# Long sums in 64-row tiles, in two passes with the row halves swapped

## The chip, the cores and the metric

The kernel runs on one core of one Trainium2 chip. Its time is that of one execution on the device, in microseconds (us); given is the median over several executions. TensorE (PE) does the matrix products, ScalarE (ACT) and VectorE (DVE) empty its results and do the rest of the arithmetic with GpSimd (POOL), and SyncE (SP) issues transfers.

## What is computed

One transformer block over 2048 tokens of width 448, with the layer norms modulated by a condition vector. All data are bf16.

```python
mod = (_silu(c) @ w_mod).reshape(...)            # six vectors of 448: sa, ca, ga, sb, cb, gb
h = _layernorm(x) * (1 + ca) + sa
q, k, v = h @ wqkv                               # 16 heads of 28
idx = pos[:, None] - 2 * arange(8)               # each token sees itself and 7 others, every second one back
attn = softmax(where(idx >= 0, q . k[idx] / sqrt(28), -1e9))
x = x + ga * ((attn . v[idx]) @ wo)
h = _layernorm(x) * (1 + cb) + sb
y = _layernorm(h)
x = x + gb * (gelu(y @ w1 + b1) @ w2 + b2)       # 448 -> 1792 -> 448
```

## The kernel before

**Tiles and stages.** The tokens lie as eight token tiles `p` of 128 partitions x 2 tokens (`NS = 2`). Tiles 0 and 1 are normalised first and go through a short start; for tiles 2 to 7 `natural_qk` (L614 to 632) computes K and then Q with the tokens on partitions, ScalarE casts the result into a staging tile `zy` (L628), and a DMA transpose issued by SP brings it into `kT` or `qT` (L631). The attention (`attention`, L678 to 797) runs over nine batches `i`: V (`pv`), the logits `lt` (L738) in two halves, the exponential `et`, the denominator `pd` (L760) and the weighted sum `po` (L771). V of batches 0 to 4 is computed straight from the normalised tokens (L706), of batches 5 to 8 from a copied window `hw`. `out_proj(p)` (L797, matmuls L803, result `pw`) is followed by the second layer norms and by a transpose into `yT` (L834). `mlp(t)` (L845 to 894) works on two token tiles at a time: w1 gives `p1` in PSUM, ScalarE's GELU (L864) writes `hm`, w2 (L883) sums 14 feature tiles into `p2`, L889 adds the residual and L893 stores. The whole is done in three phases: attention batches 0 to 4 and `mlp(0)`, batches 5 and 6 and `mlp(1)`, batches 7 and 8 and `mlp(2)` and `mlp(3)`, with work of neighbouring phases interleaved.

**Sums over 448.** The contraction of Q, K, V and w1 is 448 = 3 x 128 + 64 rows (`KT = 4` steps, `KS = 64`). `summed` (L543) adds two tasks for its items: `full`, three matmuls over all 128 rows for every item (L548), and `rest`, the half step (L554), in which two items run side by side, one on rows 0 to 63 of the array and one on rows 64 to 127 (`tile_position`). The output projection contracts 4 x 128 rows, w2 14 x 128. w1 uses `summed` for two groups `g` at a time, each with two items. On TensorE a change between such tile shapes (128 rows x 128 columns, 64 x 128, 64 x 64, 32 x 64 and so on) is called a change of tile shape below.

**What sets the order.** The program is first recorded as numbered tasks (`Plan.add`) with their dependences, and then emitted in the order of the list `ORDER`; an entry like `29:A` sends a task to another engine. `SLOTS` gives each buffer its place in the pools of `ROOM`; the PSUM pool `P` has four places of two banks. Each engine executes its instructions in the order in which they were emitted. SP carries all loads, the transposes (L527 for the normalised tokens `zT`, L631, L834) and the stores, in one sequence.

Of the kernel before, what the change touches and what calls it, by code (L numbers as in the profile page):

```python
# [14 lines left out]
S, D, H, DH, F = 2048, 448, 16, 28, 1792  # L15
KT, KS = 4, 64
# [4 lines left out]
NS = 2  # L21
SL = S // NS
LEAD = 16
# [16 lines left out]
DIRECT = range(0, 5)  # L40
ENGINE = {"A": "ACT", "D": "DVE", "P": "POOL", "R": "PE2"}
RATE = 310e3
SLOTS = [
# [10 lines left out]
85 90:A 93:P 36 114 94+3@94 82 95 113 102 92:A 91 115:D 86 103 116 96 120:A 144 97 99 104 106 117:A 135 98 118:A 142  # L54
105 119:A 145 143 133 100 146 121 136 134 126 148 137 107 147 7 127 149:D 122 138 124 150 129 139 190 123 191 140 198
141 128 125 200 199 269 130 271 236 40 270 207 33 209 38 241 201 35 237 208 210 185 211 154 39 153 242 202 152 212
151:A 8 203 187 213 238 204 159 239 214:D 205 215 186 240 155 278 206 188 279 280 156 160 307:R 161 281 243 37 282 272
192 273:A 162 157 189 171 308:D 194 172 283 193 244 218 173 195 163 219 158 275 284 196 216 285 167 217 286 447:P 246
197 164 168 165 228 174 169:D 274 309 312 276:D 277 220 313 310 314 166 221 229 225 230 311 224 222:D 247 170 315 245
176 317 316 175 226 248 233 232 318 227 290 249 289:A 319 43 287:A 223 288 320 234 250 558:P 46 45 559 321 47 231 253  # L60
345 342 346 251 560 303 482:P 44 252 324 343 322 291 561 254 323 325 347 326 344 292 304 255 293 327 348 328 373:R 256
305 294 329 257 350 258 375 52 378 376 330 340:R 53 333 379 235 377 374 296 334 331 300 41 295 351 332 259 49 335 380
299 341 336 337 297 260 382 262 301 381 349 263 261 264 338:A 383 483 352 339 384 265 484 266 449 353 267 485 385 268
# [3 lines left out]
402 452 404 443 487 453 370 490 454 444 436 455 371:D 372 456 434 491 405 488 457 493 445 459 458 492 460 435 494 461  # L67
# [3 lines left out]
513 547 515:D 599 516 564 602 568 481 569 570 604 603 571 546 605 572 548 606 573 628 607 608 574 549 635 575 550 609  # L71
612 636 577 630 637 578 610 629 640 576 579 638 581 639 611 613 580 582 641 631 583 633 586 651 614 632 587 584 585
616 588 642 615 648 617 654 646 647 618 634 652 645 656 621 649 619 644 622 620 623 643 658 650 625 624 589 626 664
590 655 627 591:A 653 657 439 592 659 556 665 662 663 674 666 660 661 669 667 675 668 678 676 679 677 686 672 673 671
687 681 670 680 690 691 694 697 693 682 688 692 685 695 683 689 701 684 698 696 709 699 710 702 711 712 705 700 703
706 704 707 708
# [77 lines left out]
def kernel(  # L154
# [14 lines left out]
    nc = tc.nc  # L169
# [3 lines left out]
    P = Plan()  # L173
    add = P.add
# [19 lines left out]
    qT = cst.tile([128, 4 * NS, WT], BF16, name="qT")  # L194
# [45 lines left out]
    first = []  # L240
# [301 lines left out]

    def summed(items, slot, reads, bufs, fills, name, after=(), split=None):  # L543
# [70 lines left out]
    def natural_qk(p):  # L614
        c0 = LEAD + 128 * p
        for half in (1, 0):
            pq = psum("pq")

            def item(s, half=half, pq=pq):
                return (lambda: pq.t[:, s, 0:D], lambda kt, rows: hT[rows, NS * kt + s, c0:c0 + 128],  # L620
                        lambda kt, rows: (wqk_st.t[:, kt] if kt < KT - 1 else wqr_st.t[rows])[:, half * D:half * D + D])
# [174 lines left out]

    def out_proj(p):  # L797
        pw = psum("pw")

        def mm():  # L800
            for s in range(NS):
                for ft in range(4):
# [160 lines left out]
```

## Time and profile before

| | |
|---|---|
| median of 3 executions | 170.32 us (169.31 to 171.79) |
| profiled execution: span | 166.6 us (its whole time is not recorded) |
| PE busy, matmuls | 160.9 us (97%), 2126 |
| PE weight loads | 83.7 us (50%) |
| DVE, ACT, POOL busy | 116.1, 102.4, 46.7 us |
| granted TensorE clock | 0.9 of full speed or more in all 40 slices |
| DMA | 18.78 MB, mean 113 GB/s |

The span is the time from the first to the last instruction of the profiled execution; the times of the executions hold what lies around it too. In the rows of the profile `L548 PE MATMUL p<-yT,w_s` is a matmul of line 548 that writes the tile `p` (buffer numbers are left out, so `p1` and `p2` read `p`) from `yT` and `w_s`; a shape `128*128 128x512` is the rows and columns of the array's tile, then the moving operand. `A <- B: 0.5, 1, 0.5` in a list of waits means that A waited for B for 0.5 us in all, once.

### The profile page before, as it was taken

What the parts mean: (1) busy time and instruction counts of PE and PEld (TensorE: products, weight loads), DVE (VectorE), ACT (ScalarE), POOL (GpSimd) and SP (SyncE); (2) the same over time, 40 slices, a digit from 0 to 9 for tenths busy, and PEclk for the clock granted to TensorE, in tenths of its full rate; (3) what the DMA queues carried; (4) which work ended last, traced back from release to release, by engine and by line L of the source; (5) the groups of instructions that cost most, each with busy time, mean ns of one, the idle gap of its engine ahead of it and who ended that gap; (6) DMA issues with size and microseconds to landing.
All of it is one profiled execution on the core that took longest, in us unless ns stands there. A gap on an engine that the chain in (4) does not pass through costs nothing.

```text
span 166.6 us, 4971 instructions
## 1 busy us (share of the span) xinstructions
PE 160.9 (97%) x2126; PEld 83.7 (50%) x2126; DVE 116.1 (70%) x271; ACT 102.4 (61%) x142; POOL 46.7 (28%) x73
## 2 busy tenths in 40 slices
PE   6999899999999999999999999999999999999992
PEld 4678544444545543445555344556434455344572
DVE  6889899958899989996938886574788930500032
ACT  3378898798489953859674468947536820097300
POOL 3136332300261201289100114700002870007200
PEclk9999999999999999999999999999999999999999
DMA  5999989799999999900091000009010026110003
GB/s 152 323 335 311 182 269 172 147 160 190 222 185 306 147 161 245 151 0 6 2 139 46 4 0 0 4 0 126 8 55 0 0 55 185 64 46 0 0 1 110
DMA packets 35573, 18.78 MB, mean 113 GB/s; under 512 B 28507, under 2 KB 34592, under 8 KB 35552
## 3 DMA queue, kind: packets, MB, share of 16 engines
q1 hardware_dynamic: 35548, 18.47, 51.0%
q8 instruction: 16, 0.26, 0.7%
q14 instruction: 5, 0.04, 0.1%
q10 hardware_dynamic: 4, 0.00, 0.0%
HBM read 9.81 MB, written 1.84 MB: 70 GB/s over the span
## 4 chain that ended last, share of the span: by engine, by line
PE 88%; DMA 4%; ACT 2%; SPq 2%; POOL 1%; DVE 1%; issue 1%
PE p L883 26%; PE p L548 22%; PE pq L548 8%; PE pw L803 8%; PE pv L706 5%; PE p L554 4%; PE lt L738 4%; PE po L771 3%; PE pv L548 3%; DMA wqk_st<-in_A_wqkv_dram 3%; PE pq L554 2%; DMA kT<-zy 2%; PE pd L760 1%; SPq L349 1%; PE pb L641 1%
## 5 line engine op out<-in xcount | busy, mean ns | idle before, releaser
L864 ACT ACTIVATE hm<-p,b_col 128x512 bf16<-128x512 f32 x56 | 33.9, 692 | 29.9 <-PE p L554 27.3
L883 PE MATMUL p<-w_s,hm 128*128 128x448 bf16 (+1 forms) x238 | 44.1, 342 | 0.0
L548 PE MATMUL p<-yT,w_s 128*128 128x512 bf16 x168 | 38.1, 380 | 0.0
L469 POOL TENSOR_TENSOR rs_all<-mvs,neg_half 128x2 f32<-128x2 f32 x22 | 16.7, 764 | 58.0 <-DVE mvs L458 57.9
L883 PEld LDWEIGHTS <-hm 128*128 128x128 bf16 x238 | 22.6, 98 | 19.3 <-issue 0.8
L889 DVE TENSOR_TENSOR x_all<-p,x1p 128x896 bf16<-128x896 f32 (+2 forms) x10 | 8.9, 902 | 25.9 <-PE p L883 25.9
L548 PEld LDWEIGHTS <-w_s 128*128 128x128 bf16 x168 | 15.8, 98 | 20.9 <-issue 2.9
L456 DVE BATCH_NORM_STATS2 stt<-x_all 128x6 f32<-128x448 bf16 x32 | 18.6, 608 | 0.8 <-DMA x_all<-in_A_x_dram 0.6
L745 ACT ACTIVATE et<-lt 128x928 bf16<-128x928 f32 x18 | 16.0, 947 | 4.2 <-PE lt L738 3.9
L841 POOL TENSOR_TENSOR x1p<-x_all,gbb_bc 128x448 f32<-128x448 bf16 x16 | 17.8, 1137 | 0.0
L548 PE MATMUL pq<-wqk_st,hT 128*128 128x448 bf16 x72 | 15.0, 354 | 0.0
L788 DVE TENSOR_TENSOR qT<-po,den 128x912 bf16<-128x912 f32 x9 | 10.0, 1106 | 6.6 <-ACT den L782 6.4
L751 DVE TENSOR_TENSOR et<-et,mask 128x928 bf16<-128x928 bf16 x18 | 11.8, 683 | 3.1 <-ACT et L745 3.0
L803 PE MATMUL pw<-wo_s,qT 128*128 128x448 bf16 x64 | 13.3, 353 | 0.0
L780 ACT ACTIVATE den<-pd 128x928 f32<-128x928 f32 x9 | 8.5, 943 | 5.9 <-PE pd L760 5.7
L819 DVE TENSOR_TENSOR h<-h,mod_bc 128x896 bf16<-128x896 bf16 x16 | 11.1, 710 | 0.3
L628 ACT CAST zy<-pq 128x896 bf16<-128x896 f32 x10 | 8.9, 912 | 1.7 <-PE pq L554 0.9
L548 PEld LDWEIGHTS <-hT 128*128 128x128 bf16 x72 | 6.4, 98 | 6.9 <-issue 1.6
L782 ACT ACTIVATE den<-den,den_bias 128x928 f32<-128x928 f32 x9 | 9.6, 1072 | 0.2
L478 DVE TENSOR_SCALAR zy<-h,mvs,rs_all 128x448 bf16<-128x448 bf16 x16 | 6.6, 457 | 4.4 <-POOL rs_all L469 4.4
L810 DVE TENSOR_TENSOR x_all<-pw,x_all 128x896 bf16<-128x896 f32 x8 | 8.7, 1086 | 1.3 <-PE pw L803 1.3
L456 DVE BATCH_NORM_STATS2 stt<-h 128x6 f32<-128x448 bf16 x16 | 9.4, 612 | 0.2
(115 smaller groups left out, 182.0 us busy)
## 6 DMA issues: line engine op xcount, KB each, us to landing
w_s<-in_B_w_dram SPq DMA_DIRECT2D x7, 224.0 KB, 3.8
out_dram<-x_all SPq DMA_DIRECT2D x7, 224.0 KB, 2.1
x_all<-in_A_x_dram SPq DMA_DIRECT2D x3, 448.0 KB, 5.3
wmod<-in_w_mod_dram SPq DMA_DIRECT2D x3, 448.0 KB, 7.2
w_s<-in_B_w_dram SPq DMA_DIRECT2D x3, 448.0 KB
wqk_st<-in_A_wqkv_dram SPq DMA_DIRECT2D x3, 225.0 KB, 3.9
wm_st<-in_w_mod_dram SPq DMA_DIRECT2D x1, 672.0 KB, 4.6
x_all<-in_A_x_dram SPq DMA_DIRECT2D x2, 224.0 KB, 2.6
```

The costliest lines, as they stand in the source:

```text
L456: add("DVE", 0.53, lambda: nc.vector.bn_stats(out=stt[:, w, b, 0:6], in_=src()), reads=reads, bufs=bufs, after=early if w == b == 0 else ( ...
L469: ways = {"POOL": (0.55 + 0.17 * n, lambda: nc.gpsimd.tensor_tensor(out=r, in0=v, in1=neg_half[:, 0:n], op=ALU.pow))}
L548: nc.tensor.matmul(out(), lhsT=lhs(kt, slice(0, 128)), rhs=rhs(kt, slice(0, 128)), start=first and kt == 0, stop=not first and kt == KT - 2)
L554: nc.tensor.matmul(out(), lhsT=lhs(KT - 1, rows), rhs=rhs(KT - 1, rows), start=first, stop=not first, tile_position=(rows.start, 0))
L745: exps.append(add("ACT", 0.83, lambda half=half, lt=lt: nc.scalar.activation(out=et.t[:, 2 * half:2 * half + 2].rearrange("p r m c -> p r ...
L751: nc.vector.tensor_tensor(out=ev, in0=ev, in1=mask[:], op=ALU.mult)
L788: nc.vector.tensor_tensor(out=qT[:, :, LEAD + q00:LEAD + q00 + 2 * WQ], in0=po.t[:, :, 0:NS * 4 * WQ].rearrange("p j (m c) -> p m j c", c=WQ),
L803: nc.tensor.matmul(pw.t[:, s, 0:D], lhsT=qT[:, KT * s + ft, LEAD + 128 * p:LEAD + 128 * p + 128], rhs=wo_s[:, ft, :], start=(ft == 0), sto ...
L819: add("DVE", 0.55, lambda vec=vec, op=op: nc.vector.tensor_tensor(out=h2.t[:], in0=h2.t[:], in1=vec.unsqueeze(1).to_broadcast([128, NS, D] ...
L841: add("POOL", 1.0, lambda n=n: nc.gpsimd.tensor_tensor(out=x1p.t[:, n, :], in0=xn(p, n), in1=gbb2_bc[:], op=ALU.add), reads=[f"x{p}", "gbb ...
L864: gelus.append(add("ACT", 0.585, lambda f=f, a=a, p1=p1s[g]: nc.scalar.activation(out=hm.t[:, f].rearrange("p n c -> p (n c)"), in_=p1.t[: ...
L883: nc.tensor.matmul(p2.t[:, n, 0:c1 - c0], lhsT=hm.t[:, f, n, q * 128:(q + 1) * 128], rhs=w2_s[:, f, c0:c1], start=(f == parts[0][0]), stop ...
```

## The change

For Q and K of token tiles 2 to 7, V of batches 5 to 8, all output projections, all of w1, and w2 of token tiles 0 to 6, every matmul now uses 64 rows. Two items share the array: in the first pass item 0 has the upper row halves and item 1 the lower ones, in the second they are swapped. Where the contraction is 448, the half step is part of the first pass (four steps, then three). Between the passes SP executes an instruction `nop`, the hop, that waits for the last matmul of the first pass, and the first matmul of the second pass waits for the hop. w1 is recorded for each group `g` alone. w2 of the last token tile stays as it was. `ORDER` is new from its third line on, `SLOTS` from the middle of its first.

```diff
+PAIRED_QK, PAIRED_V, PAIRED_WO, PAIRED_W2 = range(2, 8), range(5, 9), range(0, 8), range(0, 7)
-85 90:A 93:P 36 114 94+3@94 82 95 113 102 92:A 91 115:D 86 103 116 96 120:A 144 97 99 104 106 117:A 135 98 118:A 142
+85 90:A 93:P 36 114 94+3@94 82 95 113 102 92:A 91 115:D 86 103 116 96 120:A 144 97 99 104 106 117:A 135 7 8 105 119:A
...
+    def swapped(first, bufs, second):
+        ends = []
+        def hop():
+            nop = nc.sync.nop()
+            for mm in ends:
+                link(mm, nop)
+            ends.append(nop)
+        a = first(ends)
+        b = add("SP", 0.05, hop, needs=a, name="hop")
+        return a + second(ends, [b])
...
+    def paired(items, slot, reads, bufs, fills, name, after=(), rest=True):
+        n = KT - 1 if rest else KT
+        seen = []
+        def half(first, ends):
+            start, mm = not seen, None
+            seen.append(1)
+            for kt in range(KT if first else n):
+                for a in range(2):
+                    out, lhs, rhs = items[a if first else 1 - a]
+                    rows = slice(KS * a, KS * a + KS)
+                    mm = nc.tensor.matmul(out(), lhsT=lhs(kt, rows), rhs=rhs(kt, rows), start=start and kt == 0,
+                                          stop=not start and kt == n - 1, tile_position=(rows.start, 0))
+                    if not first and kt == a == 0:
+                        link(ends[-1], mm)
+            if first:
+                ends.append(mm)
...
-            summed([item(s) for s in range(NS)], 0.1895, [f"wqk{k}" for k in range(KT - 1)] + ["wr0", "wr1"] + [f"h{kt}_{p}" for kt in range(KT)],
+            (paired if p in PAIRED_QK else summed)([item(s) for s in range(NS)], 0.1895, [f"wqk{k}" for k in range(KT - 1)] + ["wr0", "wr1"] + [f"h{kt}_{p}" for kt in range(KT)],
...
+        if p in PAIRED_WO:
+            paired([item(s) for s in range(NS)], 0.1895, reads, [pw], [pw], f"wo{p}", rest=False)
...
-            w1_mms.extend(summed([item(g, a) for g in gs for a in range(2)], 0.2160,
...
+            for g in gs:
+                w1_mms.extend(paired([item(g, a) for a in range(2)], 0.2160, [f"w1{k}" for k in (0, 1, 2, "r0", "r1")] + [(yT, 0), (yT, 1)],
+                                     [yT, p1s[g]], [p1s[g]], f"w1_{t}_{g}", after=lts))
...
+                        for f in fs:
+                            for a in range(2):
+                                n, rows = (1 - a if up else a), slice(KS * a, KS * a + KS)
+                                mm = nc.tensor.matmul(p2.t[:, n, 0:D], lhsT=hm.t[rows, f, n, q * 128:(q + 1) * 128], rhs=w2_s[rows, f, :],
+                                                      start=done == 0 and f == fs[0], stop=done == 3 and f == fs[-1], tile_position=(rows.start, 0))
+                                if done == 2 and f == fs[0] and a == 0:
+                                    link(ends[-1], mm)
```

`link(a, b)` makes `b` wait for `a` by a semaphore. Every matmul is preceded by its weight load; there are 2650 matmuls after and 2126 before.

The first place is TensorE at the first w1, the rows in which the last output projection of the first phase (`pw`) ends and w1 begins. Before (one row of each kind; six matmuls for each `p1` on L548, two on L554):

```order
L803 MATMUL pw_1570<-wo_s_75,qT_70 128x448
L548 LDWEIGHTS w1_s_76
L548 MATMUL p1_1587<-yT_1534,w1_s_76 128x512
...
L548 MATMUL p1_1594<-yT_1534,w1_s_76 128x512
L554 LDWEIGHTS w1_r_77
L554 MATMUL p1_1613<-yT_1534,w1_r_77 128x512
...
L554 MATMUL p1_1616<-yT_1534,w1_r_77 128x512
...
L554 MATMUL p1_1587<-yT_1534,w1_r_77 128x512
...
L554 MATMUL p1_1594<-yT_1534,w1_r_77 128x512
```

After (L576 is the matmul in `paired`; eight matmuls for each `p1` in the first pass, six in the second):

```order
L576 MATMUL pw_1689<-wo_s_75,qT_70 128x448
L576 LDWEIGHTS w1_s_76
L576 MATMUL p1_1724<-yT_1632,w1_s_76 128x512
...
L576 MATMUL p1_1724<-yT_1632,w1_r_77 128x512
L576 LDWEIGHTS w1_s_76
L576 MATMUL p1_1736<-yT_1632,w1_s_76 128x512
...
L576 MATMUL p1_1748<-yT_1632,w1_r_77 128x512
L576 LDWEIGHTS w1_s_76
L576 MATMUL p1_1724<-yT_1632,w1_s_76 128x512
```

The runs over 128 rows with their remainders over 64 have become first passes of three groups and then their second passes, all in one tile shape; between the first pass of `p1_1724` and its second stand the first passes of `p1_1736` and `p1_1748`.

The second place is SP, where the first Q and K of the natural layout are made (the names behind `waits` are the semaphores that the row waits for; `zT` and `kT`/`qT` rows are the transposes, `wo_s` a load, `mod_hbm` a small transfer). Before:

```order
L527 DMA_TRANSPOSE zT_615<-zy1_97 128x8x128 [waits DMAHW4_49,DMAHW3_49,DMAHW5_49,DVE_49,Activation_49]
L527 DMA_TRANSPOSE zT_615<-zy0_96 128x8x128 [waits Pool_49]
L366 DMA wo_s_75<-in_A_wo_dram 28x4x448
L631 DMA_TRANSPOSE qT_70<-zy2_98 128x8x128 [waits DMAHW6_49,Activation_49]
L648 DMA mod_hbm_79<-mod_rows_80 4x448 [waits DMAHW7_49,Activation_49]
L631 DMA_TRANSPOSE kT_71<-zy3_99 128x8x128 [waits DMAHW0_49]
```

After:

```order
L531 DMA_TRANSPOSE zT_538<-zy0_96 128x8x128 [waits DMAHW3_49,Pool_49]
L531 DMA_TRANSPOSE zT_538<-zy1_97 128x8x128 [waits PE_49,DMAHW4_49,Pool_49]
L370 DMA wo_s_75<-in_A_wo_dram 28x4x448 [waits PE_49,DMAHW5_49]
L675 DMA_TRANSPOSE qT_70<-zy2_98 128x8x128 [waits DMAHW6_49,Activation_49]
L692 DMA mod_hbm_79<-mod_rows_80 4x448 [waits PE_49,DMAHW7_49,Activation_49]
L675 DMA_TRANSPOSE kT_71<-zy0_96 128x8x128 [waits DMAHW0_49]
```

The hop has no row of its own; it stands ahead of each row that now waits for TensorE as well (`PE_49`). Nothing else in these six rows is moved except which staging tile is transposed first.

The third place is TensorE at the first attention batches, where `pv` of batch 0 is computed. Before, one row of each run:

```order
L738 MATMUL lt_391<-qT_70,kT_71 64x58
L548 MATMUL pq_353<-hT_69,Wqk_72 128x256
L548 MATMUL pq_362<-hT_69,Wqk_72 128x256
L706 MATMUL pv_447<-Wv_74,hT_69 64x448
L738 MATMUL lt_470<-qT_70,kT_71 64x58
```

After:

```order
L782 MATMUL lt_404<-qT_70,kT_71 64x58
L782 MATMUL lt_437<-qT_70,kT_71 64x58
L592 MATMUL pq_374<-hT_69,Wqk_72 128x256
L750 MATMUL pv_483<-Wv_74,hT_69 64x448
L750 MATMUL pv_511<-Wv_74,hT_69 64x448
```

The second half of the logits (`lt_470` before, `lt_437` after) has moved ahead of the first `pv`, and one of the two Q/K runs over 128 rows that stood between the first logits and `pv` now stands ahead of the logits.

More of the change, by code (lines that the diff above doesn't have):

```diff
@@ L58 @@
[L58 to L62, printed above, removed]
@@ L541, in front_ln, with link @@
             affine(u, lambda kt: ptr[kt % 2].t[:, :, kt // 2], [(ptr[0], q) for q in range(np_)], ptr, True)
+    def swapped(first, bufs, second):
[8 more added lines that the diff above has]
+        return a + second(ends, [b])
+    def link(a, b):
+        tc.add_manual_dep(b.ins, a.ins.name, mybir.DependencyInfo(mybir.DependencyClass.Sync, mybir.DependencyReason.DATA), reason="swap")
+    def paired(items, slot, reads, bufs, fills, name, after=(), rest=True):
[14 more added lines that the diff above has]
+                ends.append(mm)
+        both = dict(reads=reads, bufs=bufs, joins=fills, mode="64x128")
+        return swapped(lambda ends: [add("PE", KT * slot, lambda: half(True, ends), instr=4 * KT, name=name + "p", after=after, **both)], bufs,
+                       lambda ends, b: [add("PE", n * slot, lambda: half(False, ends), instr=4 * n, name=name + "q", needs=b, **both)])
     def summed(items, slot, reads, bufs, fills, name, after=(), split=None):
@@ L798, in out_proj, with item @@
         pw = psum("pw")
+        def item(s):
+            return (lambda: pw.t[:, s, 0:D], lambda ft, rows: qT[rows, KT * s + ft, LEAD + 128 * p:LEAD + 128 * p + 128],
+                    lambda ft, rows: wo_s[rows, ft, :])
         def mm():
             for s in range(NS):
+                out, lhs, rhs = item(s)
                 for ft in range(4):
[L803 to L804 removed]
+                    nc.tensor.matmul(out(), lhsT=lhs(ft, slice(0, 128)), rhs=rhs(ft, slice(0, 128)), start=(ft == 0), stop=(ft == 3))
         batches = [i for i in range(NB) if i * SBQ < 128 * (p + 1) and (i + 1) * SBQ > 128 * p]
[L807 to L808 removed]
+        reads = ["wos0", "wos1"] + [f"o{i}" for i in batches]
+        if p in PAIRED_WO:
+            paired([item(s) for s in range(NS)], 0.1895, reads, [pw], [pw], f"wo{p}", rest=False)
+        else:
+            add("PE", 8 * 0.1895, mm, reads=reads, bufs=[pw], fills=[pw], instr=16, name=f"wo{p}")
         xp = x_all[:, p, :].rearrange("p (s d) -> p s d", s=NS)
@@ L890, in mlp @@
                     out=xo(xi), in0=p2.t[:, n0:n1, 0:w], in1=xo(x1p.t), op=ALU.add),
-                    bufs=[p2, x1p], reads=[(p2, n) for n in ns] + [(x1p, n) for n in ns], writes=[f"out{p}{n0}{c0}"] + ([] if last else [f"x{p}"]), name="fin")
+                    bufs=[p2, x1p], reads=[(p2, n) for n in ns if p not in PAIRED_W2] + [(x1p, n) for n in ns], writes=[f"out{p}{n0}{c0}"] + ([] if last else [f"x{p}"]), name="fin")
                 lo, hi = n0 * D + c0, (n1 - 1) * D + c1
```

69 lines of the change are left out of this document (42 added, 27 removed), and 24 rows, old and new, of tables (ORDER, SLOTS).

## The prediction

> **What bounds the kernel now.** I read the head of the page first, then the waits of the engines, then the chain that ended last in order of time.
>
> ```profile
> span 166.6 us, 4971 instructions
> PE 160.9 (97%) x2126; PEld 83.7 (50%) x2126; DVE 116.1 (70%) x271; ACT 102.4 (61%) x142; POOL 46.7 (28%) x73
> PEclk9999999999999999999999999999999999999999
> PE 88%; DMA 4%; ACT 2%; SPq 2%; POOL 1%; DVE 1%; issue 1%
> ```
>
> TensorE (PE) is busy for 160.9 of 166.6 us at a full granted clock, and 88% of the chain is its own work. What it waits for in the whole execution is a short list (columns: total us, times, longest):
>
> ```profile
> PE ps_c L382 <- DVE warm_w L242: 1.3, 1, 1.3
> PE pv L706 <- ACT qT L609: 0.5, 1, 0.5
> PE po L771 <- issue: 0.3, 1, 0.3
> PE pq L562 <- DVE Wqk L439: 0.2, 1, 0.2
> PE ps_col L410 <- ACT silu_bc L398: 0.2, 1, 0.2
> ```
>
> Only the second and the third, 0.8 us together, lie in the part whose order changes. So the time can move in three ways only: how many columns TensorE streams, what it pays between matmuls, and new waits. The chain in order of time (start, length, what), at the first w1 stage, shows what it pays between:
>
> ```profile
> 61.34 1.62 PE pw L803 x8
> 62.96 2.59 PE p L548 x12
> 65.55 0.97 PE p L554 x8
> 66.52 6.58 PE p L548 x30
> 73.10 0.75 PE p L554 x6
> 73.86 3.13 PE p L883 x16
> ```
>
> x12 without a change of tile shape ahead of it takes 2.59, which is 0.216 us per 128-row matmul of 512 columns. Eight 64-row matmuls take 0.97 and six take 0.75. The difference is 0.22 for two, so a **pair** on the two row halves costs the time of one full matmul, and what is left over is 0.97 − 4 × 0.216 = 0.10 and 0.75 − 3 × 0.216 = 0.10. The full matmuls behind a pair run have the same remainder: 6.58 − 30 × 0.216 = 0.10. With 448 columns, x16 and x8 take 3.13 and 1.62; their difference of 1.51 for eight gives 0.189 each, and 1.62 − 8 × 0.189 = 0.11. I take **0.095 us per change of tile shape**, rounded down since the rows are rounded to 0.01.
>
> **The columns streamed: no change.** The same products are done. A sum of four K steps for two items was 6 full matmuls and one pair; it is now 4 pairs, hop, 3 pairs, thus 7 slots as before. An output projection was 8 full matmuls and is 4 + 4 pairs; a w2 tile was 28 and is 14 + 14. Some 568 slots are now pairs: w1 196, w2 196, Q/K 84, output projection 64, V 28. The question is whether a pair keeps its pace in a run of up to 28 and not only of four. The rows that show pairs, and their weight loads:
>
> ```profile
> L554 PE MATMUL p<-yT,w_r 64*128 64x512 bf16 x56 | 7.4, 379 | 0.0
> 64.96 0.60 PE L548 MATMUL p<-yT,w_s 128*128 128x512 bf16 x2
> 65.48 0.55 PEld L554 LDWEIGHTS <-w_r 64*128 64x128 bf16 x8 [0.42 <-DMA w_s<-in_B_w_dram]
> 65.49 1.04 PE L554 MATMUL p<-yT,w_r 64*128 64x512 bf16 x8
> 66.45 0.76 PEld L548 LDWEIGHTS <-w_s 128*128 128x128 bf16 x5 [0.42 <-issue]
> ```
>
> The eight loads, 0.55 us of them, lie inside the 1.04 us in which the matmuls run, so twice as many loads add nothing there. From both sides: rounding of 0.97 and 0.75 leaves a pair between 0.21 and 0.23, which over 568 pairs is −3 to +8 us; the low end is excluded, since 0.216 is what the full rows need to stream the same columns. I take 0, the value that the runs of three and of four share.
>
> The Trainium skill, page "TensorE: Matmul & The Clock Gate", Part 3, says that a weight load overlaps with matmuls in flight only when its row group differs. Here the next load on a row half follows a matmul on that same half, so by this rule each pair would expose one load; the trace disagrees already before (30 full matmuls on the same rows in 6.58 us, loads inside).
>
> **Changes of tile shape: fewer.** Counted in the two orders on TensorE there are 79 changes of tile shape before and 69 after. Up to the first w1 they go from 51 to 48, from there on from 28 to 21: the 128-row runs and their remainders alternated 34 times, and 14 such changes are left, but Q/K, V and output projections are now 64-row blocks between other shapes, which takes part of this back. 10 × 0.095 = **−0.95 us**. Both ends: 0 if the changes fall where TensorE waits anyway, −1.1 with 0.11 each.
>
> **The two waits.** Where they sit in the chain:
>
> ```profile
> 17.11 0.91 ACT qT L609
> 18.03 0.04 issue
> 18.07 1.64 PE pv L706 x16
> 19.71 0.37 PE lt L738 x30
> 37.15 0.48 PE po L771 x56
> 37.63 0.34 issue
> 37.98 0.77 PE po L771 x72
> ```
>
> The V products of the first attention batch wait for a PSUM buffer that ScalarE empties at 18.03. In the new order the second half of the logits, which came after them at 19.71, stands ahead of those products: 0.37 of the 0.5 us is filled. The hole inside `po` has no releaser; it stands where two `po` met, and these are now apart. I take **−0.7 us**, 0.37 and 0.34; ends 0 (something else is late next, above all the layer-normed tile that the first natural-layout Q/K needs) and −0.8.
>
> **The hops: 59 new waits** (12 at Q/K, 4 at V, 8 at the output projection, 28 at w1, 7 at w2). A hop is an instruction on SyncE (SP) that waits for the last matmul of pass 1, and the first matmul of pass 2 waits for it. No row shows one. The nearest rows are a hand-over from TensorE through ScalarE to SP, and SP's own semaphore instruction:
>
> ```profile
> 28.28 0.25 PE pd L760 x8
> 28.53 0.02 issue
> 28.56 0.95 ACT den L780
> 29.51 0.14 SPq L648
> 29.64 0.05 issue
> L631 SPq EVENT_SEMAPHORE  x5: 17/17/17, 26.8 to 48.4; - x5
> ```
>
> Handing over costs 0.02 to 0.05 us each way, the instruction 0.02 to 0.14; and a matmul's result comes later than its slot ends, by a mean of 379 − 216 = 0.16 us. An idle SP thus needs 0.16 + 0.02 + 0.02 to 0.14 + 0.05, or 0.25 to 0.37 us; I take **0.3**. Between a pass 1 and its own pass 2 the new order puts other matmuls at every hop: at the least three slots (0.57 us of 448 columns, 0.65 of 512) or the logits, mostly 0.65 to 0.9, at w2 1.1 to 3. So with SP idle all 59 are covered; without that cover they would cost 59 × 0.3 = 18 us.
>
> But SP works in order, and a hop stands behind what SP issues before it:
>
> ```profile
> L631 SPq DMA_TRANSPOSE qT<-zy x6: 1303/1448/2123, 26.9 to 66.3; - x6
> L631 SPq DMA_TRANSPOSE kT<-zy x6: 1237/1284/2470, 29.7 to 63.8; - x6
> 34.69 2.47 SPq L631 DMA_TRANSPOSE kT<-zy  x1
> 37.22 4.20 SPq L631 DMA_TRANSPOSE qT<-zy  x2
> SPq L834 <- DVE zy L491: 40.2, 2, 26.0
> SPq L893 <- DVE x_all L889: 29.3, 5, 16.6
> ```
>
> A transpose holds SP for 1.24 to 2.47 us. 17 of the 59 hops stand directly behind one, 10 behind a plain transfer, 32 behind another hop. Of the 17, ten have a cover of 1 us or less, and eight of these lie in the stretch up to 67 us, where SP issues nearly without pause; later SP mostly sits waiting (40.2 and 29.3 us). Ends: 0 if every transpose is through before pass 1 ends; if each of the ten is released just as pass 1 ends, 1.36 (the middle of the two medians) + 0.3 − 0.7 of cover = 0.96 each, 9.6 us. I followed the new order by hand with the durations above: the input of a transpose is ready well before the pass 1 that follows, except at about four places with 0 to 0.3 us to spare. I take 0.1 at each of these, **+0.4**, nearer to the low end. The other direction counts too: SP now stands at a hop until pass 1 is through, and what is queued behind it, transposes and weight loads, goes out later. Up to 62 us these have slack of about the cover itself; I add nothing.
>
> The rest is moved without a price: at w1 the GELUs of a group can now start after each pass 2 rather than two groups later, and ScalarE at 61% is not what TensorE waits for in any row above. The last token tile's w2 keeps its full-row form, so the end itself is unchanged.
>
> **The sum.** 166.6 − 0.95 − 0.7 + 0.4 = 165.35 us of span, 1.25 less. The profiled execution's whole time isn't shown; the median of the three runs, 170.32, is 3.7 above its span, and I keep that offset: **169.1 us**. The runs of before spread from 169.31 to 171.79, and 2% (3.4 us) is about what can be told from no change, so this counts as the same.
>
> **The rivals.**
> (a) *SP and TensorE in lockstep*, slower. Hops behind transposes come late, pass 2 waits, the evacuation and the next transpose are late in turn. For it: ten hops with a cover below one transposition, a stretch in which SP hardly rests. Against it: the transposes are released by ScalarE work that lies before the pass 1 in question. Price 0.55 to 0.96 at ten hops, 5.5 to 9.6, less the 1.65 saved: 174.2 to 178.3, say 175.5. It decides from 0.5 us per place on.
> (b) *Pairs lose pace in long runs*: at 0.226 a pair, near the top of what the rounding leaves, 568 × 0.010 = +5.7, about 174.7. Its extreme: a load can't start before the matmul on its own rows has ended, and every pair exposes one; a load takes 98 ns,
>
> ```profile
> L883 PEld LDWEIGHTS <-hm 128*128 128x128 bf16 x238 | 22.6, 98 | 19.3 <-issue 0.8
> ```
>
> so 568 × 0.098 = 56 us, about 225; the 6.58 us for 30 speak against it.
> (c) *The change does not do what it says*: changes of shape are saved, but waits reappear elsewhere and the hops take the 1.65 us saved, so it stays at 170.3.
> (d) *More is gained*: the changes of shape go at 0.11, the waits go, and the hops are free, with a gain in the order of other engines' work as well. From −1.9 to −3.7, so 166.6 to 168.4.
>
> **How the numbers follow.** Forecast 0.52 (its own range 167.9 to 170.1), (c) 0.18, (d) 0.14, (a) 0.12, (b) 0.03, the exposed loads 0.01. Faster by over 2% means below 166.9: the end of (d), with the spread of a median of few runs, 0.10. Slower means above 173.7: (a), (b) and the exposed loads, 0.16. The rest, 0.74, is within. The range takes in most of (d) and the beginning of (a), 166.4 to 174.0; what lies outside is about 0.06 below and 0.13 above.
>
> **What would show it.** Switches: runs of pairs in the chain with the remainder 0.10 only at their ends, and w1 pieces of 4 and 3 slots adding up to 0.216 per pair. The two waits: no `pv` waiting for ScalarE near 18 us, the first w1 at about 62.4 rather than 62.96. Hops: waits of TensorE on SP, a list that is empty now; under 1 us in all bears out the forecast, over 5 us is (a), and then they stand before 67 us behind transposes. Pace: the mean distance of paired matmuls in w2. I am wrong if SP's issues run later than I followed by hand, or if the new order starves TensorE through a PSUM buffer that ScalarE has not emptied.

## The result, and the profile after

The changed kernel takes **176.92 us** (median of 4, 175.50 to 182.31) beside 170.95 us for the kernel before (4 runs, 169.31 to 171.79): a ratio of **1.0396, 95% interval 1.0339 to 1.0453**. (Some executions run in a slower state, such as the one of 182.31 us with a mean granted clock of 0.962; the ratio is formed without them, so it is not the quotient of the two medians.) It is 4% slower, where 169.1 us was forecast and 174.0 was the upper end of the range. The head of the page of the changed kernel, with its chain by engine:

```profile
span 175.4 us, 6080 instructions
PE 160.8 (92%) x2650; PEld 85.3 (49%) x2650; DVE 119.2 (68%) x270; ACT 103.1 (59%) x145; POOL 49.5 (28%) x72
PEclk9999999999999999999999999999999999999997
PE 42%; DVE 21%; POOL 11%; DMA 9%; SPq 8%; issue 3%; ACT 3%; POOLq 0%; ACTq 0%
```

TensorE is busy for as long as before (160.8 us, 160.9 before), but the span is 8.8 us longer. On the chain that ended last its share fell from 88% to 42%; VectorE and GpSimd, 2% together before, have 32%. The waits of TensorE, whose list held 0.8 us of such waits before (here and below without the one for `warm_w` at the start, 1.3 us in every kernel, and without other waits before 14 us):

```profile
PE pq L576 <- ACT hT L508: 2.5, 2, 2.2
PE pq L576 <- SPq L552: 1.6, 1, 1.6
PE p L939 <- SPq L552: 1.5, 1, 1.5
PE po L815 <- DVE et L795: 1.2, 1, 1.2
PE pd L804 <- DVE et L795: 0.7, 1, 0.7
PE lt L782 <- DVE zy L673: 0.4, 1, 0.4
```

L552 is the hop; two of 59 were waited for. To add it up I took TensorE's start-to-start distances after 14 us, less the time that the columns need (by this measure the waits of the list are 0.1 to 0.2 us longer: 1.36 at `po`, 0.88 at `pd`, 1.8 and 1.7 at the hops). Single gaps over 0.23 us make 1.2 us before and 9.6 after; the changes of tile shape that stand at none of these gaps 70 x 0.100 = 7.0 us before and 55 x 0.096 = 5.3 after. (In all, the traces have 71 changes after 14 us before and 61 after, 79 and 69 in the whole execution; six of the 61 stand at gaps and are counted there.) So the last matmul should start 8.4 − 1.7 = 6.7 us later; it starts at 170.6 us instead of 163.4, 7.2 later, and 0.5 is left over. After the last matmul, the span had 1.6 us more in this execution, because the last store took 3.1 us to land instead of 1.5; in all other traces, of either order, the span ends 3.2 to 3.3 us after the start of the last matmul, as before.

Where the wait of the third row, 1.5 us at the hop near 144 us, comes from is seen in the chain there (start, length, what):

```profile
139.49 0.70 POOL rs_all L473
140.22 2.13 DVE zy L482 x2
142.38 0.91 DVE zy L495
143.28 1.39 DVE zy L482 x2
...
145.95 0.20 SPq L885
...
146.27 2.82 PE p L939 x28
149.09 10.58 PE p L576 x98
```

TensorE waits for the hop, the hop stands on SP behind the transpose of yT (L885), the transpose waits for the normalised rows `zy`, and these take VectorE 2.13 us for two, where one takes 0.39 otherwise. What GpSimd does at that time:

```profile
140.14 4.08 POOL L892 TENSOR_TENSOR x1p<-x_all,gbb_bc 128x448 f32<-128x448 bf16 x4
```

The other hop that was waited for, near 36 us, stood behind a transpose that held SP for 3.00 us, where the prediction took 1.36:

```profile
34.76 3.00 SPq L531 DMA_TRANSPOSE zT<-zy  x1
```

### The profile page after: what moved, and what is told of

The parts are those of the page before. It is cut to its first block, busy times and chain, and to the rows that moved or that the text cites. A ratio compares the mean times of both kernels' runs of the same rounds, so it can differ in the third digit from the quotient of the medians.

```text
span 175.4 us, 6080 instructions
## 1 busy us (share of the span) xinstructions
PE 160.8 (92%) x2650; PEld 85.3 (49%) x2650; DVE 119.2 (68%) x270; ACT 103.1 (59%) x145; POOL 49.5 (28%) x72
## 4 chain that ended last, share of the span: by engine, by line
PE 42%; DVE 21%; POOL 11%; DMA 9%; SPq 8%; issue 3%; ACT 3%; POOLq 0%; ACTq 0%
PE p L576 9%; PE p L939 9%; DVE stt L460 5%; PE pq L576 5%; PE pw L576 5%; POOL x1p L892 5%; POOL rs_all L473 4%; DVE zy L482 3%; DMA x_all<-in_A_x_dram 3%; DVE h L870 3%; PE p L957 3%; DMA zT<-zy 3%; DMA b_bc<-in_B_b_dram 3%; PE pv L750 3%; PE po L815 3%
## 5 line engine op out<-in xcount | busy, mean ns | idle before, releaser
L576 PE MATMUL p<-yT,w_s 64*128 64x512 bf16 x336 | 41.7, 376 | 0.0
L939 PE MATMUL p<-w_s,hm 64*128 64x448 bf16 x392 | 39.7, 350 | 1.5 <-SPq L552 1.5
L473 POOL TENSOR_TENSOR rs_all<-mvs,neg_half 128x2 f32<-128x2 f32 x21 | 15.9, 764 | 55.0 <-DVE mvs L462 54.8
L939 PEld LDWEIGHTS <-hm 64*128 64x128 bf16 x392 | 18.3, 94 | 19.5 <-SPq L552 2.0
L576 PEld LDWEIGHTS <-w_s 64*128 64x128 bf16 x336 | 16.4, 94 | 19.5 <-SPq L552 0.3
L576 PE MATMUL pq<-wqk_st,hT 64*128 64x448 bf16 x144 | 17.1, 350 | 4.2 <-ACT hT L508 2.5
L576 PE MATMUL pw<-wo_s,qT 64*128 64x448 bf16 x128 | 14.0, 349 | 0.1
L576 PEld LDWEIGHTS <-hT 64*128 64x128 bf16 x168 | 7.8, 94 | 11.2 <-ACT hT L508 2.9
L482 DVE TENSOR_SCALAR zy<-h,mvs,rs_all 128x448 bf16<-128x448 bf16 x16 | 9.2, 614 | 3.1 <-POOL rs_all L473 3.1
L576 PE MATMUL p<-yT,w_r 64*128 64x512 bf16 x56 | 10.6, 376 | 0.0
```

What stands on the lines that cost most here:

```text
L473: ways = {"POOL": (0.55 + 0.17 * n, lambda: nc.gpsimd.tensor_tensor(out=r, in0=v, in1=neg_half[:, 0:n], op=ALU.pow))}
L482: add("DVE", 0.31, lambda: nc.vector.tensor_scalar(out=dst(), in0=src(), scalar1=mvs[:, w, b, 0:1], scalar2=rs_all[:, w, b:b + 1], op0=ALU ...
L576: mm = nc.tensor.matmul(out(), lhsT=lhs(kt, rows), rhs=rhs(kt, rows), start=start and kt == 0, stop=not start and kt == n - 1, tile_positi ...
L939: mm = nc.tensor.matmul(p2.t[:, n, 0:D], lhsT=hm.t[rows, f, n, q * 128:(q + 1) * 128], rhs=w2_s[rows, f, :], start=done == 0 and f == fs[0 ...
```

## The experiments

Two theories stood against each other first. H: the hops cost the time, directly and by holding SP up. O: the hops cost little, and it is the new order of the work on all engines. Each kernel was timed beside the kernel before on the same chip.

**Without hops, and with hops that nobody waits for.** In the second pass the row halves aren't swapped, so no hop is needed.

```diff
-                    out, lhs, rhs = items[a if first else 1 - a]
+                    out, lhs, rhs = items[a]
...
-            nop = nc.sync.nop()
-            for mm in ends:
-                link(mm, nop)
-            ends.append(nop)
+            pass
```

> The changed kernel with its order and its 64-row pairs, but the second pass keeps the row halves of the first (it multiplies the upper half of item 0 and the lower half of item 1 again, so half of each paired sum is left out and half counted twice), and there is no hop. Theory H (the hops on SyncE cost the time): the 1.6 and 1.5 us that TensorE waited directly for hops go, and with SyncE free the later waits for VectorE near 86, 117 us shrink too; 168 to 171 us. Theory O (the new order of the other engines' work and the tail cost it, the hops little): only the two direct waits go, 173 to 175 us, with the first paired Q/K still starting near 24 us and the span still ending over 4 us after the last matmul.

The other keeps the hop on SP, and only takes the link from hop to matmul away (same first two lines):

```diff
-                    if not first and kt == a == 0:
-                        link(ends[-1], mm)
```

> As the kernel without hops (second pass on the same row halves, so the sums are not those wanted), but SyncE still executes the 59 hop instructions, each waiting for the last matmul of its first pass; TensorE waits for none. It tells the two sides of a hop apart. If TensorE's wait is the cost, it runs like the kernel without hops, within 0.5 us. If SyncE held up at the hops is the cost (transposes and loads go out later), it runs like the changed kernel, 175 to 177 us, or at least 2 us above the one without hops.

Measured: 1.0452 (1.0337 to 1.0567) without hops, 1.0418 (1.0291 to 1.0546) with hops on SP alone. Neither is faster than the changed kernel at 1.0396, so **H falls**: taking the hops away gains nothing. O did not forecast this well either: 176.35 us were measured without hops, above its 173 to 175, the first paired Q/K starts at 22.55 us and not near 24, and the late end of the span is gone. Without the hops the waits of TensorE are

```profile
PE po L810 <- issue: 2.9, 1, 2.9
PE pq L573 <- ACT hT L508: 1.6, 2, 1.3
PE po L810 <- DVE et L790: 1.2, 1, 1.2
PE p L573 <- DMA yT<-zy: 0.8, 1, 0.8
PE pd L799 <- DVE et L790: 0.7, 1, 0.7
```

Near 144 us TensorE now waits for yT itself, 0.8 us, so of the 1.5 us at the hop there about half had only been handed on. The waits for `et` are the same to 0.1 us. Near 36 us, where the changed kernel stood 1.6 us at a hop, a wait without a releaser has come, and 2.9 us long:

```profile
34.71 0.54 PE L573 MATMUL pq<-wqk_st,hT 64*128 64x448 bf16 x4
35.18 0.56 PE L810 MATMUL po<-et,vb 64*32 64x57 bf16 x50
38.63 0.24 PE L810 MATMUL po<-et,vb 64*32 64x57 bf16 x14 [2.89 <-issue]
```

With hops that nobody waits for it is 3.1 us, at the same matmul. It lies in the middle of 64 matmuls with the same operands, so data can hardly be what is missing. A 16 KB packet of the instruction queue ran from 36.2 to 37.1 us; TensorE went on 1.5 us after it. Both traces of before have such a hole at the same matmul, the 607th (0.5 and 1.0 us by start-to-start distances), also 1.4 us after the end of an instruction packet. So without hops TensorE saves 3.1 us of waits at them and loses at least as much at this hole, at yT, and to a fall of the clock that is shown further down; what the hops alone cost can't be read from these two kernels.

**Pairs alone, in the order of before.** `full` and `rest` of before with 64-row pairs on fixed halves, no hops:

```diff
+            if pairs:
+                for i in range(0, len(items), 2):
+                    for k in range(2 * KT - 2):
+                        kt = k % (KT - 1)
+                        for a in range(2):
+                            out, lhs, rhs = items[i + a]
+                            rows = slice(KS * a, KS * a + KS)
+                            nc.tensor.matmul(out(), lhsT=lhs(kt, rows), rhs=rhs(kt, rows), start=first and k == 0,
+                                             stop=not first and k == 2 * KT - 3, tile_position=(rows.start, 0))
+                return
```

> The kernel before with its own order and no hop, but the same sums in 64-row pairs without a swap (natural Q/K, V of batches 5 to 8, all output projections, w1, w2 of token tiles 0 to 6; each row half is used twice in place of both halves, so the sums are not those wanted). Changes of tile shape go from 79 to 55. If a pair keeps the pace of one full matmul in long runs and a change of shape costs 0.095 us: 24 x 0.095 = 2.3 us less where TensorE is the bound, 168 to 169 us. If pairs lose 10 ns each in long runs: 5.7 us more, about 174.

Measured: 1.0033 (0.9979 to 1.0087). The pairs as such cost nothing, and the 24 saved changes of shape, 2.3 us, did not arrive either; what took them back was not settled. Its one trace, of the slowest of its ten executions, has a hole of 2.2 us without a releaser near 60 us, 1.4 us after an instruction packet, where the traces of before have none; whether its faster executions have it is not known.

**The kernel before again.**

> The kernel before, unchanged, for a second trace of it: how much the start varies between executions (arrival of the token tiles and of the first transposed tile zT, at 11.7 and 20.3 us in the first trace, against 12.3 and 23.1 us in the changed kernel). Theory O-start: the start of the changed kernel is later by its order, so this trace shows zT again near 20.3 us. Rival: it is the spread of the loads, and zT lands anywhere between 20 and 23 us here.

Its first zT was worked on at 20.0 us (20.3 before), in the changed kernel at 23.1 and without hops at 21.6. That looks like O-start, but all the traces together don't decide it: in the five of the old order zT is first worked on at 19.7 to 22.1 us (21.5 in the pairs without a swap, 22.1 in the shifted kernel below, where TensorE waits 1.4 us for it), in the nine of the new order at 20.7 to 23.6, and in three of these nine TensorE doesn't wait for it. It is later on the average in the new order; the rival, a spread between executions, is not excluded. The first paired Q/K starts at 24.06 and 22.55 us, before at 22.3: the two logits runs that were put ahead of `pv` brought TensorE there earlier only to wait.

**Is it the instruction fetch?** The two holes at `et` also end about 1.2 us after an instruction packet. So all later instructions of TensorE were shifted by splitting or joining the warm-up matmuls at the very start, in the changed kernel both ways, and in before:

```diff
-        for _ in range(n):
-            nc.tensor.matmul(t.sums[0].t[:, 0, 0:256], lhsT=warm_w[:, 0:128], rhs=warm_w[:, 0:256], start=True, stop=True)
+        for k in range(2 * n):
+            nc.tensor.matmul(t.sums[0].t[:, 0, 0:128], lhsT=warm_w[:, 0:128], rhs=warm_w[:, 0:128], start=True, stop=True)
```

> The changed kernel with 35 more matmuls on TensorE ahead of everything: each of the 35 warm-up matmuls of 256 columns becomes two of 128, the same streaming time. All later instructions of TensorE stand 70 places further back in its instruction stream; nothing else is changed. Theory F (TensorE runs out of instructions: the holes of 1.36 us inside `po` near 86 us and 0.88 us ahead of `pd` near 117 us end 1.1 and 1.2 us after a 16 KB instruction fetch, and stand where the stream crosses a block of instructions): both holes leave their matmuls (the 1498th and 2040th of the stream of before this edit), and others may stand elsewhere, always 1 to 1.5 us behind the end of such a fetch. Theory D (the matmuls there wait for VectorE's `et`, as the profile names it): the holes stay at the same matmuls with the same lengths within 0.3 us. The hole ahead of the hop near 144 us stays by both. 174 to 177 us by F, 176 to 178 by D.

The joined form:

```diff
+        for k in range((n + 1) // 2):
+            w = 512 if 2 * k + 1 < n else 256
+            nc.tensor.matmul(t.sums[0].t[:, 0, 0:w], lhsT=warm_w[:, 0:128], rhs=warm_w[:, 0:w], start=True, stop=True)
```

> The changed kernel with 16 fewer matmuls ahead: pairs of warm-up matmuls of 256 columns become one of 512. TensorE's later instructions stand 32 places further forward. By theory F the holes near 86 and 117 us move or change their length, and a new one may come; by theory D both stay. 174 to 178 us by F, 176 to 178 by D.

And the split form in the kernel before:

> The kernel before with the same 35 matmuls more ahead. Its hole inside `po` (0.5 us in the first trace, 1.0 in the second, both at the 607th matmul, 1.4 us after a fetch ended) leaves its place by theory F, and the time stays within 1.5 us of before (167 to 171): with 128-row matmuls TensorE uses up instructions half as fast, and few holes are to be had. If this hole had to do with the data, it stays at the same `po`.

Measured: 1.044 (1.0299 to 1.058), 1.0535 (1.0462 to 1.0609) and 0.9994 (0.9955 to 1.0033). In the first the hole ahead of `pd` stayed at its matmul, the 2075th now (2040 + 35), 0.7 us long in the profile's list as it was (0.88 and 0.90 by start-to-start distances):

```profile
PE p L939 <- DVE w_s L705: 2.0, 1, 2.0
PE pq L576 <- ACT hT L508: 1.6, 2, 1.3
PE p L939 <- SPq L552: 1.5, 1, 1.5
PE pd L804 <- DVE et L795: 0.7, 1, 0.7
PE po L815 <- issue: 0.6, 1, 0.6
```

The one inside `po` near 86 us is gone, which D had not forecast; but 5 us earlier TensorE waited 2.0 us for VectorE (`w_s`, the scaling of w2), which would leave `et` ready by then. The joined form shows the same: `pd` waits 0.7 us for `et` at the 2023rd (17 matmuls were taken away, so 2040 − 17), and ahead of the lost hole at `po` stands a wait of 2.5 us for `w_s`. **For the hole at `pd` theory F was wrong and the name that the profile gave was right**, and the packet beside it was chance; for the one at `po` that is argued. The joined form is also the slowest, 179.84 us, above what either theory said: the clock fell twice in its trace, and its four executions have a mean clock of 0.981.

In before with the shift, the hole at the 607th matmul is gone:

```profile
38.38 1.31 PE L771 MATMUL po<-et,vb 64*32 64x57 bf16 x111
```

For the holes that the profile puts to "issue", F fits. That trace alone would not show it, since TensorE had waited 1.4 us for the first Q/K there. The joined form says more:

```profile
PE pq L577 <- issue: 2.7, 1, 2.7
```

It is the 606th matmul of the stream, 1.4 us after a packet, and now a matmul of Q/K: the hole has kept its place in TensorE's stream and not its operation. The same order with 128-row matmuls:

```diff
+            if first and rest:
+                for a in range(2):
+                    out, lhs, rhs = items[a]
+                    ...
+            out, lhs, rhs = items[0 if first else 1]
+            for kt in range(n):
+                nc.tensor.matmul(out(), lhsT=lhs(kt, slice(0, 128)), rhs=rhs(kt, slice(0, 128)), start=not rest and kt == 0, stop=kt == n - 1)
```

> The order, buffers and passes of the changed kernel, without hops, but with 128-row matmuls: the first pass makes the two half steps and all full steps of item 0, the second the full steps of item 1. 2126 matmuls instead of 2650, and 146 changes of tile shape instead of 69, which alone is 77 x 0.095 = 7.3 us more. Theory F: the holes behind instruction fetches (5.3 us in the kernel without hops) shrink to 1 us or less. What is left of waits, by the first Q/K for the transposed tile, by `lt` near 55 us and for yT near 146 us, is the order's own: 2 to 4 us. If the holes of 3, 1.4 and 0.9 us stand at the same places with half the instructions, F falls. About 176 to 180 us.

One execution: 176.55 us. Its hole is at the 607th matmul once more (here one of `pd`), 1.25 us, against 3.06 in the pairs without hops (1.1 and 2.9 in the profile's lists). That half the instructions make it smaller is not shown by this: the pairs without hops and without `x1p`, below, have 1.5 there. Waits for `et` and yT are gone, and so is that for zT. With its 77 more changes of shape TensorE is busy for 167.4 us, 6.6 more than in the changed kernel, and the other engines keep up with that: they lack a few us, not more.

**GpSimd beside VectorE.** The last theory, V: `x1p` on GpSimd and the layer norm on VectorE get in each other's way.

```diff
-            add("POOL", 1.0, lambda n=n: nc.gpsimd.tensor_tensor(out=x1p.t[:, n, :], in0=xn(p, n), in1=gbb2_bc[:], op=ALU.add),
+            add("POOL", 1.0, lambda: None,
...
-                    out=xo(xi), in0=p2.t[:, n0:n1, 0:w], in1=xo(x1p.t), op=ALU.add),
+                    out=xo(xi), in0=p2.t[:, n0:n1, 0:w], in1=xo(xi), op=ALU.add),
```

> The changed kernel without the 16 additions `x1p` on GpSimd (L892, 17.8 us; w2's bias is left out of the output, the final addition takes `x_all` itself). Theory V (in the new order VectorE's chain of layer norms meets `x1p` on GpSimd, and both slow each other: the normalisation of L482 takes 0.39 us alone and 1.10 us beside `x1p` in the changed kernel's trace; VectorE and GpSimd are late at the `et`, `yT` that TensorE needs): the waits of TensorE for `et` near 86 and 117 us (1.36 and 0.88 us) and for the hop behind yT near 144 us (1.7 us) shrink, together by 3 us or more; 173 to 174 us. Rival S (these waits come from where TensorE's work stands in the order, whatever GpSimd does): they shrink by less than 1 us; 176 to 178 us.

> The control: the kernel before without `x1p` in the same way. In its trace no wait of TensorE leads back to `x1p`, and L478 takes 0.39 us beside GpSimd as alone, so by theory V and by its rival nothing changes: within 1 us of before. If it is faster by as much as the changed kernel without `x1p`, that one's gain says nothing of the change.

> Both taken away from the changed kernel: no hops (second pass on the same row halves, so the sums are not those wanted) and no `x1p`. By theory V and the finding that hops cost nothing on their own, what is left is the instruction-fetch hole near 36 us (3 us and a lower clock after it) and the wait at the first Q/K (1.5 us): 171 to 173 us, with no wait for `et` or yT over 0.5 us. If it is as fast as before (169 to 170), hops and `x1p` were all of the cost; if it stays at 175 or more, the cause is elsewhere.

Measured: the changed kernel 172.31 us, **1.0215 (1.0150 to 1.0280)**, so about 3 us of the loss are gone; before 1.0043 (1.0005 to 1.0082), no gain; without hops as well 173.72 us, 1.0301 (1.0240 to 1.0362), no further gain and a little above its forecast. The normalisation of the rows for yT, first in the kernel before, then in the changed one, then in the one without `x1p` (ns, min/median/max):

```profile
L478 DVE TENSOR_SCALAR zy<-h,mvs,rs_all x16: 385/392/1101, 54.6 to 134.9; 128x448 bf16<-128x448 bf16 x16
```

```profile
L482 DVE TENSOR_SCALAR zy<-h,mvs,rs_all x16: 350/394/1155, 60.1 to 144.3; 128x448 bf16<-128x448 bf16 x16
```

```profile
L482 DVE TENSOR_SCALAR zy<-h,mvs,rs_all x16: 355/391/398, 60.9 to 140.5; 128x448 bf16<-128x448 bf16 x16
```

The mean is 457 ns before and 614 after (page, groups). So the expectation for the control was wrong in saying that the normalisation takes 0.39 us beside GpSimd before: of its 16, two fall beside `x1p` and take 0.73 and 1.10 us; after, five do and take 1.10 to 1.16. The other eleven take 0.35 to 0.40, also beside GpSimd's other work. The four of them near 140 us and their copies, which took 4.6 us beside `x1p`, took 1.8 without, and these waits of TensorE remain:

```profile
PE pq L576 <- SPq L552: 1.7, 1, 1.7
PE pq L576 <- ACT hT L508: 1.5, 2, 1.2
PE p L939 <- DVE w_s L705: 0.4, 1, 0.4
PE lt L782 <- DVE zy L673: 0.4, 1, 0.4
```

Those for `et` and for the hop near 144 us are gone. **V holds** in that `x1p` is the cause of these waits. The Trainium skill, page "SBUF — State Buffer", section "Who interferes with whom", says that VectorE's copies and scalar operations in their fast two-port modes and GpSimd take turns on one pair of ports, each blocking the other for a whole instruction; the 0.39 and 1.10 us agree with it.

Taking `x1p` away takes two things away at once, though: the slower VectorE beside it, and `x1p`'s place in GpSimd's own sequence, ahead of `rs_all`, the small operation that every normalisation needs. Near 86 us it is the second that shows in the changed kernel:

```profile
83.89 1.43 POOL L892 TENSOR_TENSOR x1p<-x_all,gbb_bc 128x448 f32<-128x448 bf16 x1
85.29 1.47 POOL L473 TENSOR_TENSOR rs_all<-mvs,neg_half 128x2 f32<-128x2 f32 x2
86.02 0.70 DVE L482 TENSOR_SCALAR zy<-h,mvs,rs_all 128x448 bf16<-128x448 bf16 x2 [1.42 <-POOL rs_all L473]
```

`rs_all` starts when `x1p` ends, VectorE stands for 1.42 us (0.41 without `x1p`), the two normalisations take their usual 0.70, and the `et` that TensorE lacks is behind them. (The order of before has such a stand too, 1.49 us near 79 us, but no TensorE that waits for what comes behind it.) Near 117 and 140 us it is the first: normalisations of 1.10 to 1.16 us. How the 3 us divide between the two was not measured.

**The stretch before 40 us.** My guess was that what is left, 1.0215, lies there. The kernel without `x1p` was given Q/K in 128-row matmuls, without hops there (the lines as in the kernel with full rows):

> The changed kernel without `x1p` (w2's bias left out) and with the 12 Q/K sums of the natural layout in 128-row matmuls: first pass both half steps and item 0, second pass item 1, no hop there; everything else keeps its pairs and hops. 72 matmuls fewer, 90 changes of tile shape instead of 69 (21 x 0.095 = 2.0 us more). It tells what the 3 us left in the kernel without `x1p` are. Theory E (the stretch before 40 us: TensorE stands 1.8 us at the hop behind a transpose, or 1.6 to 3.1 us without hops because 64-row matmuls use up its instructions before the next fetch lands, and the granted clock then falls to 0.5 for 3.4 us, 1.7 us more): the wait near 36 us is 1.3 us or less as in the kernel with full rows, and no run shows the clock at 0.99; 172.3 + 2.0 - 0.8 - 1.7 = about 171.8 us. Rival (the 3 us are spread over the later stages): the clock and the wait do not matter, 174.3 us.

Measured: 173.63 us, 1.0229 (1.0146 to 1.0313), between the 171.8 and 174.3 of the two theories: **not decided**. The wait near 36 us is gone from its trace, of its slowest execution, as E said, but TensorE waits 2.2 us for the first transposed tile and the clock falls there instead, for 6.8 us; and of its other three executions the one at a full clock is the slowest (mean clocks 0.988, 0.998 and 1.0 with 173.29, 172.27 and 173.97 us).

A last thing cost time in part of the executions. In the kernel without hops, after the hole of 2.9 us, the granted clock (last figure but two of each row) falls:

```profile
35.00:38.50 3.50, 0.74 (x54) 0.44 (x50) 0.64 (x1) 2.18 (x3) 0.00 (x0) 1.00 1.19 117
38.50:42.30 3.80, 3.67 (x34) 1.65 (x36) 3.05 (x5) 0.00 (x0) 0.00 (x0) 0.55 0.61 133
42.30:46.00 3.70, 3.70 (x104) 2.01 (x100) 1.67 (x3) 3.18 (x4) 0.00 (x0) 1.00 0.77 39
```

The trace gives 0.5 for 3.4 us, so 1.7 us lost. The kernel without `x1p` has the same after its 1.7 us at the hop, and all its four runs have a mean clock of 0.99, as has one of the changed kernel's four. In the changed kernel's own trace the clock did not fall until the very end, though TensorE waited 2.2 and 1.6 us. The Trainium skill, page "TensorE: Matmul & The Clock Gate", Part 1, has the half clock and the window of 3.4 us after an idle window; here 1.7 us of waiting were enough, so a full idle window was not needed.

The kernel without hops and without `x1p` shows what these things are worth together. Its profiled execution is one in which the clock stayed full and TensorE did not wait for zT; after 14 us its longest waits are

```profile
PE po L810 <- issue: 1.5, 1, 1.5
PE pd L799 <- ACT den L819: 0.8, 1, 0.8
```

Its span is 168.8 us, its time 171.22. Its other executions, with mean clocks of 0.98 and 0.99, have spans of 171.3 to 173.0, and the kernel before on the same chip mostly 166.2 to 168.6. So with hops and `x1p` away, and in an execution without the fall of the clock, most of the loss is gone. That is one execution, and its second pass leaves the row halves as they are.

## Why the prediction was wrong

- **Columns and pace: right.** 98 paired matmuls of w1 take 10.58 us, 0.216 per pair, and TensorE's busy time did not move. The rival of slower pairs and that of the exposed loads are out.
- **Changes of tile shape: right.** The traces have the 79 and 69 changes that were counted, at 0.096 to 0.100 us each where TensorE doesn't wait: about −1.0, and −0.95 was the term. (The −1.7 above is more because six changes stand at gaps.) But ten changes fewer did not make the kernel faster, nor did 24 fewer in the order of before.
- **The two waits, −0.7: wrong.** The wait for ScalarE went, and zT, named there as what could be late next, was late by more: TensorE waits 2.2 and 0.3 us for `hT`, which is made from it, against 0.5 us for ScalarE before. I had taken nearly the upper end of that term instead of following zT to its landing. How much of this is the order and how much the spread of zT between executions stays open.
- **The hops, +0.4: mis-sized in the trace.** Two were waited for, 3.1 us. That the kernel is no faster without hops does not make the term right; it is luck: in place of the one near 36 us, behind a transpose of 3.00 us, came a fetch hole of 2.9, and the other handed on a late yT, in part.
- **"The rest is moved without a price": this step failed.** It checked ScalarE and not VectorE and GpSimd. I followed the order by hand with durations of before, in which `zy` mostly takes 0.39 us; in the new order `x1p` falls beside it five times of 16 (two before), where it takes 1.10 or more, and ahead of `rs_all` on GpSimd, and yT and `et` come late. Some 3 of the loss of about 6.7 us are this: 1.0396 with `x1p`, 1.0215 without, and no gain from the same edit in the order of before.
- **The offset, +3.7: wrong, but without weight.** In most runs whose span is known the time is span + 1.7 us (in some up to 2.95). By that, and this is an estimate, before's profiled execution took some 168.3 us and was a short one. Since the forecast is in effect the median of before less 1.25 us, the offset drops out of the difference: −1.25 was forecast, about +6.7 came, 8 us apart.
- **The rival (a), lockstep of SP and TensorE, 174.2 to 178.3**, has the measured time in its range, but by luck and not by its mechanism: it called for stalls at ten hops, most of them before 67 us, and there was one there, and one near 144 us.
- **Missing as a rival:** 64-row tiles need more instructions, 2650 matmuls with their weight loads instead of 2126. Holes of 1.5 to 3.1 us that fit the fetch show in the kernels without hops, and one of 2.7 in the joined form, against 0.3 to 0.9 in before.

Of the remaining 2%, about half of the loss, the traces show the early wait for zT, the stand at about 36 us, and the clock after it; that these are all of it was not shown, and its cause stays open.

## What to carry to other kernels

Where one engine fills 97% of the span, a new order must be walked on every engine, and with the durations that it makes: an operation's time depends on what stands beside it on the engine that shares its port, and on what stands ahead of the small operations that it needs. When a wait shows behind a hand-over such as the hop, take the hand-over away in an experiment before it is blamed, and look in the trace at what comes in its place before it is acquitted. And a gap without a releaser, in the middle of like instructions, is worth comparing with the instruction packets; where a gap has a named releaser, as at `pd` here, a packet beside it can be chance.

## What was unexpected on the chip

- A VectorE normalisation of 128 x 448 takes 0.39 us alone or beside other GpSimd work, and mostly 1.10 to 1.16 beside GpSimd's `x1p`, about as long as that one takes (mostly 1.03 to 1.07).
- TensorE's instructions come in packets of 16 KB (16 of them before, 21 after); at the holes that fit a lack of them, it goes on 1.2 to 1.5 us after the packet.
- 1.7 us of waiting can halve the granted clock for the next 3.4 us (no `x1p`), and 2.2 us need not (changed kernel).
- In nine of the 14 traces a hole without a releaser, 0.2 to 3.1 us, stands at the 606th or 607th matmul of TensorE's stream, at `po`, `pd` or Q/K as the order has it. In three of the other five TensorE had just stood at a hop.
